# A long convolution and a linear attention on one core: transposes moved to DMA, paired 64-channel tails, and a new order of the work

## The chip, the core and the metric

The kernel runs on one core of a Trainium2 chip. The core has five engines with queues of their own: TensorE (PE in the profile, its weight loads PEld), VectorE (DVE), ScalarE (ACT), GpSimd (POOL) and SyncE (SP), which here only issues DMA. The metric is the device time of one execution in microseconds; less is better.

## The reference

Two independent blocks on 2048 positions and 576 channels, in bfloat16, whose outputs stand side by side in the last dimension.

```
# block A: a gated long convolution
k_shift = sum over t < 4 of k[s - t] * shift_k[:, t]
kv = k_shift * v
y = irfft(rfft(kv padded to 2S) * rfft(ssm_k padded to 2S))[:S] + kv * ssm_D
outA = q * y

# block B: linear attention with 32 heads of 18 channels
q, k, v = split(x @ wqkv)
phi(t) = where(t > 0, t + 1, exp(t)) + 1e-6
kv = einsum("bhsd,bhse->bhde", phi(k), v);  z = sum of phi(k) over s
o = einsum("bhqd,bhde->bhqe", phi(q), kv) / (phi(q) . z + 1e-6)
outB = o @ wo
```

## The kernel before

One string, `ORDER`, lists some 280 units of work, and the program issues them in that order. Each engine executes its own instructions in the order of issue, so the string fixes every engine's queue; semaphores hold an instruction back until its data and its buffers are there. A unit is a name with arguments and, last, the letters of the engines that take its elementwise steps (A for ACT, D for DVE, P for POOL): `cv.0.3.PDD` is convolution chunk 0, step 3, with its multiplication on POOL and the two other steps on DVE. All PSUM tiles share one pool of four buffers of two banks, taken in rotation.

Block A works in five chunks of channels (`ACH`: four of 128, one of 64).

- `hl` loads a chunk of the filter `ssm_k`; `hT` (L443) turns it with 16 TensorE transposes into PSUM, evicts it and adds `ssm_D` into row 0 (L448).
- `cv` (L427 to L433) is the four-tap shift convolution, elementwise in SBUF, and its product with v.
- A long DFT is split in two factors. `h1` and `u1` (L460) multiply by the tables G (filter and signal), evicted into Ch and Cu. `ht` and `ut` (L467) turn these by DMA into Cth and Ctu. `h2` and `u2` (L483) are the short factor, evicted into T and SU.
- `pX` and `pT` (L493, L495) are the complex product of the two spectra on DVE, whole tiles of 128 x 2048 with both inputs in SBUF.
- `i1` (L507) is the short inverse factor: two planes of T and two of X are multiplied by small tables W and added in PSUM, from two row halves. `i2` (L520, L521) is the long one with the tables F, and is multiplied by q on eviction (L522). F is G turned: `FT` (L529) is 16 TensorE transposes and an eviction for each of the two. `st` stores the result.

Block B works in four groups of 512 positions and 16 rows of 128 positions.

- `xd` loads x turned, by DMA transposes; `xl` loads it straight, for G below.
- `k` and `q` (L397, L406) are the projections followed by phi (L389 on ACT, L390 on DVE). q is kept turned, in five channel chunks `HCH` of whole heads: four of 126 channels, one of 72.
- `G` (L570) is x^T phi(k), 32 matmuls for each of five units; `kv` (L583) multiplies it by the weights of v and masks it to blocks of heads; `M` (L601) multiplies that by wo.
- `den` (L610) gives the denominators for all positions, and 1/den is taken on DVE. `bc` (L635) spreads 1/den over the channels by a matmul with a selection matrix (`es` makes it, masked for each group), and DVE multiplies q by it.
- `o` (L644) multiplies q by M: per row, five chunks, each a matmul of 512 and one of 64 columns; ACT evicts, and one DMA per row stores.

At the start `io`, `iw`, `wk`, `ix`, `sin`, `sw` compute index tables and sines; `wu.40` is 40 matmuls on zeros; `hc` makes masks on POOL.

Of the kernel before, what the change touches and what calls it, by code (L numbers as in the profile page):

```python
# [25 lines left out]

ACH = [(0, 128), (128, 128), (256, 128), (384, 128), (512, 64)]
# [3 lines left out]
wm io wu.0 ix.0 sin.1 id ix.1 hl.0 iw wk wu.40 sin.0 hT.0.D FT.1.D h1.0.0.0.A h1.0.1.0.A FT.0.D h1.0.1.1.A  # L31
h1.0.0.1.A iv sw W lw.0 xd.2 q.2.0 hc lw.1 k.8 q.2.2 q.2.1 ls Wj hl.1 hT.1.D k.9 k.11 k.10 h1.1.1.0.D xd.0 k.3
kl.0 cv.0.0.D one h1.1.0.0.A k.1 ht.0.0 h2.0.0.0.A h2.0.0.1.A eps cv.0.1.DD cv.0.2.DD q.0.1 h1.1.1.1.A q.0.0
h1.1.0.1.A xd.3 q.3.0 q.0.2 vl.0 cv.0.3.PDD k.2 cv.1.0.P k.0 ht.0.1 h2.0.1.1.A q.3.1 k.12 u1.0.1.1.A k.15
h2.0.1.0.D ht.1.1 h2.1.1.0.A k.13 u1.0.0.1.A hl.2 hT.2.D u1.0.0.0.A cv.1.1.PD k.14 xd.1 u1.0.1.0.A xl.2
cv.1.2.DD cv.1.3.DPP ht.1.0 xl.1 h2.1.1.1.A q.1.1 h2.1.0.1.A h2.1.0.0.A q.1.0 q.1.2 h1.2.1.0.A ut.0.1 k.7
u2.0.1.0.D u2.0.1.1.A k.6 h1.2.0.1.A k.4 ut.0.0 u2.0.0.1.D u2.0.0.0.A k.5 pX.0.0 pT.0.0 u1.1.1.0.A u1.1.1.1.A
q.3.2 u1.1.0.1.A xl.0 xl.3 kl.1 pX.0.1 pT.0.1 u1.1.0.0.A es G.0 vl.1 h1.2.0.0.A h1.2.1.1.A cv.2.0.D cv.2.1.DD
cv.2.2.DD G.2 ut.1.0 G.4 u2.1.0.1.D u2.1.0.0.A ut.1.1 i1.0.0.1.A hl.3 i1.0.0.0.A i1.0.1.1.A i1.0.1.0.A
cv.2.3.DDD ql.0 cv.3.0.D cv.3.1.DD u2.1.1.1.A ht.2.0 u2.1.1.0.A pX.1.1 pT.1.1 hT.3.A G.1 lwv pX.1.0 pT.1.0  # L40
h2.2.0.1.A ht.2.1 G.3 cv.3.2.DD u1.2.0.0.A i2.0.0 kl.2 u1.2.1.1.A u1.2.1.0.A kv u1.2.0.1.A i2.0.1 h2.2.0.0.A
h2.2.1.0.A den h2.2.1.1.A i1.1.1.0.A lwo M.0 i1.1.0.1.A i1.1.0.0.A i1.1.1.1.D ut.2.0 u2.2.0.0.A M.2 ut.2.1
# [23 lines left out]
def _warm(tc, psum, K, n):  # L66

    nc = tc.nc
    zero = K.sm[:, 1984:2048].bitcast(BF)
    if n:  # L70
        ps = psum.tile([128, 128], FP32, name="warm_ps", tag="big")
        for _ in range(n):
            nc.tensor.matmul(ps[:], lhsT=zero, rhs=zero, start=True, stop=True)
    else:
        nc.vector.memset(zero, 0.0)


def _head_consts(tc, cpool, K):
# [8 lines left out]
    K.hmask = cpool.tile([128, 7], FP32, name="hmask")  # L87
    nc.gpsimd.memset(K.hmask[:], 1.0)
    nc.gpsimd.affine_select(out=K.hmask[:], in_=K.hmask[:], compare_op=ALU.is_ge, fill=0.0, base=0,
                            pattern=[[-18, 7]], channel_multiplier=1)  # L90
    nc.gpsimd.affine_select(out=K.hmask[:], in_=K.hmask[:], compare_op=ALU.is_ge, fill=0.0, base=17,
                            pattern=[[18, 7]], channel_multiplier=-1)

    K.esel = cpool.tile([128, 5, 126], BF, name="esel")
    nc.gpsimd.memset(K.esel[:], 1.0)
    for j in range(4):
        e = K.esel[32 * j:32 * (j + 1)]
        nc.gpsimd.affine_select(out=e, in_=e, compare_op=ALU.is_ge, fill=0.0, base=0,
                                pattern=[[126, 5], [1, 126]], channel_multiplier=-18)
        nc.gpsimd.affine_select(out=e, in_=e, compare_op=ALU.is_ge, fill=0.0, base=17,  # L100
                                pattern=[[-126, 5], [-1, 126]], channel_multiplier=18)
    K.jmask = cpool.tile([128, 4], FP32, name="jmask")
    nc.gpsimd.memset(K.jmask[:], 0.0)
    for j in range(4):
        nc.gpsimd.memset(K.jmask[32 * j:32 * (j + 1), j:j + 1], 1.0)
# [126 lines left out]
def kernel(  # L232
# [24 lines left out]
    psum = ctx.enter_context(tc.tile_pool(name="psum", bufs=4, space=PSUM))  # L257
# [4 lines left out]

    def slot8(shape, dt, name):

        return c8.tile(shape, dt, name=name, tag="c8", bufs=2)

    def slotv(shape, dt, name):

        return c8.tile(shape, dt, name=name, tag="vq", bufs=2)
# [62 lines left out]
    Wall = slotv([128, D, 4], BF, "Wall")  # L332
    Wj = lpool.tile([128, 4, D], BF, name="Wj")
    pqT = lpool.tile([128, 5, S], BF, name="pqT")
    pk = big.tile([128, 16, D + 1], BF, name="pk", tag="pk")

    def load_shift():
        nc.sync.dma_start(out=Wall[:].rearrange("p d j -> p (d j)"),
                            in_=A_shift_k.rearrange("d j -> (d j)").partition_broadcast(128))

    def shift_w():
        nc.scalar.activation(out=Wj[:], in_=Wall[:].rearrange("p d j -> p j d"), func=ACT.Copy)
# [8 lines left out]
    def load_g(key, src, gi):  # L351
        d0, dn = GRP[gi]
        n = 19 if key == 'k' else 16
        if gi == 2:
            t = lpool.tile([128, n, dn], BF, name=key, tag="tail", bufs=2)
# [22 lines left out]
    def h_load(ci):  # L378
        d0, dc = ACH[ci]
        s = st.setdefault(ci, {})  # L380
        s['h'] = slot4([128, S], BF, "h_sb", "h", 2)
# [10 lines left out]
    def b_k(r):  # L392
        ps = psum.tile([128, 1024], FP32, name="k_ps", tag="big")
# [7 lines left out]
    def b_q(g, pair):  # L401
        ps = psum.tile([128, 2, 512], FP32, name="q_ps", tag="big")
        for j, c in enumerate(pair):
            h0, hn = HCH[c]
            for t in range(5):
                nc.tensor.matmul(ps[0:hn, j, :], lhsT=wqk[:, t, h0:h0 + hn], rhs=xT[g][:, t, :],  # L406
                                 start=(t == 0), stop=(t == 4))
        n = len(pair)
        hn = HCH[pair[0]][1]
        phi(ps[0:hn, 0:n, :], pqT[0:hn, pair[0]:pair[0] + n, g * 512:(g + 1) * 512], hn)  # L410
# [25 lines left out]
    def h_T(ci, eng='D'):  # L436
        d0, dc = ACH[ci]
        s = st[ci]
        h = s['h']
        ps = psum.tile([128, 16, 128], BF, name="hT_ps", tag="big")  # L440
        hv = h[0:dc, :].rearrange("d (a b) -> d b a", b=16)
        for b in range(16):
# [282 lines left out]
```

## Time and profile before

| | |
|---|---|
| median of three runs | 172.44 us (171.57 to 173.75) |
| the profiled execution, first to last instruction | 170.0 us |
| what lies around the span (median less span; the page gives the profiled execution no other time) | 2.4 us |
| PE busy | 159.0 us, 2176 matmuls |
| DVE busy | 139.7 us |
| ACT busy | 122.8 us |
| POOL busy | 70.9 us |
| DMA | 32.58 MB, mean 192 GB/s |

Busy time is the share of the span in which an engine works on something; a busy PE need not be at its peak, since matmuls overlap. An engine's idle time matters only where the end of the program waits for it.

### The profile page before, as it was taken

To read this page: it belongs to the slowest core of one execution; us is meant where nothing else is said; L and a number is where in the kernel's file an instruction comes from. 1 tells how busy PE (TensorE), PEld (TensorE's weight loads), DVE (VectorE), ACT (ScalarE), POOL (GpSimd) and SP (SyncE) were. 2 spreads that over 40 slices of the span, in tenths; PEclk is the share of its full clock that TensorE was granted. 3 is DMA by queue.
4 is the path that set the end of the run, shared out by engine and by line. 5 is a ranking of instruction groups with operands and counts; after the bars stand their busy time and mean duration, and the time that the engine had idled before them with its cause. 6 is when DMAs were issued, how large, how long until landed. Compare 5 with 4: busy or idle time off the path is not lost.

```text
span 170.0 us, 4984 instructions
## 1 busy us (share of the span) xinstructions
PE 159.0 (94%) x2176; PEld 106.9 (63%) x2176; DVE 139.7 (82%) x159; ACT 122.8 (72%) x142; POOL 70.9 (42%) x76
## 2 busy tenths in 40 slices
PE   4779999999999799999999999999999999999990
PEld 4768566665575456565685586857856765677750
DVE  7995589998989867999599887997999777999530
ACT  3458987977788899923597477989897778784431
POOL 7998982027693397000000049999900400000000
PEclk9999999999999999999999999999999999999997
DMA  5999699799989999999998655980959957988685
GB/s 147 273 268 250 119 267 136 137 272 225 145 183 217 263 178 318 290 213 219 306 214 196 106 150 40 182 159 18 146 126 276 202 128 69 237 180 258 191 244 117
DMA packets 81704, 32.58 MB, mean 192 GB/s; under 512 B 57432, under 2 KB 80978, under 8 KB 81682
## 3 DMA queue, kind: packets, MB, share of 16 engines
q1 hardware_dynamic: 81682, 32.26, 91.0%
q8 instruction: 17, 0.28, 0.7%
q14 instruction: 5, 0.04, 0.1%
HBM read 15.48 MB, written 4.72 MB: 119 GB/s over the span
## 4 chain that ended last, share of the span: by engine, by line
PE 77%; DMA 11%; DVE 6%; ACT 3%; issue 0%; ACTq 0%
PE q_ps L406 12%; PE g_ps L570 12%; PE k_ps L397 11%; PE o_ps L644 10%; PE s_ps L460 8%; PE i_ps L507 8%; DMA Ctu<-Cu 7%; PE s_ps L483 5%; DMA Cth<-Ch 4%; PE hT_ps L443 2%; PE i_ps L520 2%; PE i_ps L521 2%; PE bc_ps L635 1%; PE kv_ps L583 1%; DVE mp L138 1%; DVE mp L139 1%
## 5 line engine op out<-in xcount | busy, mean ns | idle before, releaser
L429 POOL TENSOR_TENSOR at<-k,Wj 128x2048 bf16<-128x2048 bf16 (+1 forms) x5 | 16.4, 3289 | 36.3 <-DVE at L430 36.2
L406 PE MATMUL q_ps<-xT,wqk 128*126 128x512 bf16 (+1 forms) x100 | 23.3, 381 | 0.0
L644 PE MATMUL o_ps<-wo_M,pqT 126*128 126x512 bf16 (+3 forms) x160 | 21.9, 286 | 0.0
L397 PE MATMUL k_ps<-wqk,xT 128*128 128x512 bf16 (+1 forms) x160 | 21.8, 286 | 0.0
L460 PEld LDWEIGHTS <-G 128*128 128x128 bf16 x320 | 17.6, 98 | 5.2 <-issue 2.1
L570 PE MATMUL g_ps<-pk,x_sb 128*128 128x512 bf16 (+3 forms) x160 | 20.4, 286 | 0.0
L277 ACT ACTIVATE Cu<-s_ps 128x1024 bf16<-128x1024 f32 (+1 forms) x18 | 16.6, 951 | 2.8 <-PE s_ps L460 2.4
L397 PEld LDWEIGHTS <-xT 128*128 128x128 bf16 x160 | 11.4, 98 | 11.1 <-issue 1.1
L644 PEld LDWEIGHTS <-pqT 126*128 126x128 bf16 (+1 forms) x160 | 11.2, 97 | 10.7 <-issue 0.8
L406 PEld LDWEIGHTS <-wqk 128*126 128x126 bf16 (+1 forms) x100 | 12.5, 131 | 8.2 <-issue 1.2
L277 ACT ACTIVATE Ch<-s_ps 128x1024 bf16<-128x1024 f32 (+1 forms) x18 | 16.3, 952 | 1.4 <-PE s_ps L460 0.8
L507 PE MATMUL i_ps<-W,T 64*128 64x128 bf16 x288 | 16.6, 216 | 0.4 <-DVE pqT L638 0.4
L649 ACT ACTIVATE ob<-o_ps 128x576 bf16<-128x576 f32 x16 | 10.4, 653 | 8.9 <-PE o_ps L644 8.7
L570 PEld LDWEIGHTS <-x_sb 128*128 128x128 bf16 (+1 forms) x160 | 10.8, 101 | 9.5 <-issue 0.2
L507 PE MATMUL i_ps<-W,X 64*128 64x128 bf16 x288 | 16.5, 216 | 0.0
L277 ACT ACTIVATE T<-s_ps 128x1024 bf16<-128x1024 f32 x16 | 15.8, 1021 | 0.6 <-PE s_ps L483 0.6
L277 ACT ACTIVATE V<-i_ps 128x1024 bf16<-128x1024 f32 x14 | 13.6, 1027 | 2.8 <-PE i_ps L507 2.1
L390 DVE SCALAR_TENSOR_TENSOR pqT<-pqT,q_ps 126x1024 bf16<-126x1024 bf16 (+1 forms) x12 | 12.2, 1037 | 3.8 <-ACT pqT L389 3.8
L522 DVE TENSOR_TENSOR q<-i_ps,q 128x1024 bf16<-128x1024 f32 (+1 forms) x10 | 11.2, 1116 | 4.6 <-PE i_ps L521 4.6
L389 ACT ACTIVATE pqT<-q_ps,neg 126x1024 bf16<-126x1024 f32 (+1 forms) x12 | 11.6, 968 | 4.3 <-PE q_ps L406 4.3
L430 POOL TENSOR_TENSOR at<-at 128x2048 bf16<-128x2048 bf16 (+1 forms) x4 | 12.4, 3094 | 5.4 <-DVE at L429 5.2
L433 POOL TENSOR_TENSOR v<-at,v 128x2048 bf16<-128x2048 bf16 (+1 forms) x3 | 10.3, 3419 | 9.8 <-DVE at L430 9.6
(120 smaller groups left out, 335.4 us busy)
## 6 DMA issues: line engine op xcount, KB each, us to landing
x_sb<-in_B_x_dram SPq DMA_DIRECT2D x4, 576.0 KB
out_dram<-ob SPq DMA_DIRECT2D x16, 144.0 KB, 4.0
h_sb<-in_A_ssm_k_dram SPq DMA_DIRECT2D x4, 512.0 KB
k<-in_A_k_dram SPq DMA_DIRECT2D x2, 1024.0 KB, 9.1
v<-in_A_v_dram SPq DMA_DIRECT2D x2, 1024.0 KB, 6.6
q<-in_A_q_dram SPq DMA_DIRECT2D x2, 1024.0 KB
out_dram<-q SPq DMA_DIRECT2D x2, 1024.0 KB
wqk<-in_B_wqkv_dram SPq DMA_DIRECT2D x2, 576.0 KB
```

The lines of the kernel that those rows point to most:

```text
L277: nc.scalar.activation(out=out, in_=in_, func=ACT.Copy)
L389: nc.scalar.activation(out=out_ap, in_=ps_ap, func=ACT.Exp, bias=K.neg1[0:n, :])
L390: nc.vector.scalar_tensor_tensor(out=out_ap, in0=out_ap, scalar=1.0, in1=ps_ap, op0=ALU.min, op1=ALU.max)
L397: nc.tensor.matmul(ps[:, n0:n1], lhsT=xT[r // 4][:, t, rr * 128:(rr + 1) * 128], rhs=wqk[:, t, D + n0:D + n1], start=(t == 0), stop=(t == 4))
L406: nc.tensor.matmul(ps[0:hn, j, :], lhsT=wqk[:, t, h0:h0 + hn], rhs=xT[g][:, t, :], start=(t == 0), stop=(t == 4))
L429: on[0].tensor_tensor(out=t_, in0=kk[:, 3 - stage:19 - stage], in1=wb(stage), op=ALU.mult)
L430: on[1].tensor_tensor(out=a_, in0=a_, in1=t_, op=ALU.add)
L460: nc.tensor.matmul(ps[:, bi, 0:dc], lhsT=K.G[ri][:, b, :], rhs=xf(b), start=True, stop=True)
L507: nc.tensor.matmul(ps[:, r, g, :], lhsT=s[key, hf][64 * r:64 * r + 64, z, x, 128 * g:128 * g + 128], rhs=K.W[64 * r:64 * r + 64, m, :], st ...
L522: nc.vector.tensor_tensor(out=qs, in0=ps[:, :, 0:dc], in1=qs, op=ALU.mult)
L570: nc.tensor.matmul(ps[0:fn, n0:n1], lhsT=x_sb[:, r, f0:f0 + fn], rhs=pk[:, r, n0:n1], start=(r == 0), stop=(r == 15))
L644: nc.tensor.matmul(ps[:, n0:n1], lhsT=pqT[0:hn, c, r * 128:(r + 1) * 128], rhs=B['M'][0:hn, c, n0:n1], start=(c == 0), stop=(c == 4))
```

## The change

It has seven parts.

1. **Transposes by DMA.** The two tables F are G turned by a DMA transpose. Filter chunks 1 to 4 are first copied with their axes swapped (new unit `hp`, on POOL for chunks 1, 3 and 4 and on ACT for chunk 2) and then turned by a DMA transpose; chunk 0 keeps the TensorE transposes.
2. **128-channel chunks of q.** q lies in four chunks of 128 channels and a tail of 64. The tails of two groups of positions share one tile of 128 partitions (`pq4`, unit `qt`): groups 2 and 0, and 3 and 1.
3. **Paired output.** `o` computes two rows at once; the tails of the two rows use the two halves of the partitions. One DMA stores both rows, and each row's eviction has an engine letter.
4. **32-row 1/den tiles.** `bc` reads only the 32 rows of 1/den that belong to a group of positions, and two groups sit on different row groups of TensorE; one unit `bt` serves the tails. The masked selection matrices (`es`) are gone.
5. **M with 128-channel chunks.** Heads cross chunk borders, so each of four chunks of M gets a second small product (`kvx`).
6. **Pre-subtracted products.** `pS` subtracts the second plane of T from the first, so that `i1` reads three planes and not four. It is used for chunks 2 and 3 (POOL three times, DVE once). `pX` and `pT` may run on POOL: seven of the 18 products do.
7. **Order and buffers.** `ORDER` is new throughout, and the digits behind a slash now name the PSUM buffer and the slots of SBUF rings that a unit takes, in place of a rotation. x for group 0 is the first load, then the weights; masks (`hc`) are made in the middle.

```diff
-    def b_q(g, pair):
-        for j, c in enumerate(pair):
-            h0, hn = HCH[c]
+    def b_q(g, half):
+        for j in range(2):
+            c = 2 * half + j
             for t in range(5):
-                nc.tensor.matmul(ps[0:hn, j, :], lhsT=wqk[:, t, h0:h0 + hn], rhs=xT[g][:, t, :],
+                nc.tensor.matmul(ps[:, j, :], lhsT=wqk[:, t, 128 * c:128 * c + 128], rhs=xT[g][:, t, :],
                                  start=(t == 0), stop=(t == 4))
...
+    def b_qt(p):
+        ps = psum.tile([128, 512], FP32, name="qt_ps")
+        for t in range(5):
+            for i, g in enumerate(PAIR[p]):
+                nc.tensor.matmul(ps[64 * i:64 * i + 64, :], lhsT=wqk[:, t, 512:576], rhs=xT[g][:, t, :],
+                                 start=(t == 0), stop=(t == 4))
+        phi(ps[:], pq4[:, p, :], 128)
...
+    def h_perm(ci, eng='P'):
+        s['hp'] = slot4([128, 16, 128], BF, "hp", "h", 3)
+        hv = s['h'][0:dc, :].rearrange("d (a b) -> d b a", b=16)
+        if eng == 'A':
+            nc.scalar.activation(out=s['hp'][0:dc], in_=hv, func=ACT.Copy)
+        else:
+            (nc.gpsimd if eng == 'P' else nc.vector).tensor_copy(out=s['hp'][0:dc], in_=hv)
+
+    def h_T(ci, eng='T'):
+        if eng == 'T':
+            s['hT'] = slot4([128, 16, 128], BF, "hT", "h", 3)
+            nc.sync.dma_start_transpose(out=s['hT'][:, :, 0:dc], in_=s['hp'][0:dc].rearrange("d b a -> d (b a)"))
+        else:
...
-    def prod(ci, hf, key):
+    def prod(ci, hf, key, eng='D'):
+        e = nc.gpsimd if eng == 'P' else nc.vector
...
+            a = t if key == 'S' else s['X', hf]
+            e.tensor_tensor(out=a[:, :, 0, :], in0=a[:, :, 0, :], in1=a[:, :, 1, :],
+                            op=ALU.subtract if key == 'S' else ALU.add)
...
+        planes = [('T', 0, 0)] + [('T', 1, 1)] * ('S' not in done) + [('X', 0, 2)] + [('X', 1, 2)] * ('A' not in done)
...
-        for b in range(16):
-            nc.tensor.transpose(out=ps[:, b, :], in_=K.G[ri][:, b, :], identity=K.ident[:])
-        evict(K.F[ri][:], ps[:], eng)
+        nc.sync.dma_start_transpose(out=K.F[ri][:], in_=K.G[ri][:].rearrange("p b k -> p (b k)"))
...
+        for i in range(2):
+            j = 2 * gg + i
+            q = slice(32 * j, 32 * j + 32)
+            nc.tensor.matmul(ps[:, i, :], lhsT=K.esel[q, 128 * c:128 * c + 128], rhs=B['rden'][q], start=True, stop=True)
...
+    def b_out(p, rr, eng='AA'):
+        rs = [4 * g + rr for g in PAIR[p]]
...
+        for n0, n1 in ((0, 512), (512, 576)):
+            for i in range(2):
+                h = slice(64 * i, 64 * i + 64)
+                nc.tensor.matmul(pss[i][:, n0:n1], lhsT=pq4[h, p, rr * 128:(rr + 1) * 128], rhs=B['M'][h, 4, n0:n1],
+                                 start=False, stop=True)
+        for i, r in enumerate(rs):
+            evict(B['ob'][:, r, 0:D], pss[i][:, 0:D], eng[i])
```

The new order, from the masks to the end of block A's third chunk, reads (each unit's buffers behind the slash):

```diff
+h2.1.0.1.D/31 h2.1.0.0.D/0 lwv hT.2.T/2 ut.1.1/0 G.4/20 pT.0.1.P h1.2.1.0.A/13 ut.1.0/1 h1.2.1.1.A/1 h1.2.0.0.A/0
+cv.3.0.D FT.1 pT.0.0.D pS.1.1.N cv.3.1.PD wom kv/23 h1.2.0.1.A/1 ql.0/1 u2.1.1.0.A/10 u2.1.0.1.D/02 u2.1.0.0.A/3 den/1
+u2.1.1.1.A/0 i1.0.1.0.A/02 i1.0.0.0.A/3 i1.0.0.1.A/0 ht.2.1/1 i1.0.1.1.A/2 h2.2.1.0.A/13 pX.1.1.D/0 cv.3.2.PP ht.2.0/0
...
+hT.3.T/0 h2.2.0.1.A/01 h2.2.0.0.A/2 i2.0.0/3 h1.3.1.1.A/01 lwo bc.3.1/0 M.0.A/2 ut.2.0/1 h1.3.1.0.A/3 h1.3.0.1.D/1
+pT.1.1.P h1.3.0.0.A/2 M.3.D/0 u2.2.0.0.A/13 hl.4/21 ut.2.1/0 bc.1.1/1 pT.1.0.P u2.2.0.1.A/2 bt/0 M.4.A/3 M.1.A/1
+cv.3.3.DDD M.2.A/2 u2.2.1.1.A/03 u2.2.1.0.A/0 ht.3.1/1 ht.3.0/0 i1.1.1.1.D/11 i1.1.0.0.A/2 i1.1.1.0.A/3 hp.4.P/1
...
```

293 lines of the change are left out of this document (158 added, 135 removed).

## The prediction

> **What bounds the kernel now.** I read the page from the top: busy time by engine, the 40 slices, the DMA queues, the chain that ended last.
>
> ```profile
> span 170.0 us, 4984 instructions
> PE 159.0 (94%) x2176; PEld 106.9 (63%) x2176; DVE 139.7 (82%) x159; ACT 122.8 (72%) x142; POOL 70.9 (42%) x76
> PEclk9999999999999999999999999999999999999997
> GB/s 147 273 268 250 119 267 136 137 272 225 145 183 217 263 178 318 290 213 219 306 214 196 106 150 40 182 159 18 146 126 276 202 128 69 237 180 258 191 244 117
> DMA packets 81704, 32.58 MB, mean 192 GB/s; under 512 B 57432, under 2 KB 80978, under 8 KB 81682
> PE 77%; DMA 11%; DVE 6%; ACT 3%; issue 0%; ACTq 0%
> ```
>
> PE is busy 94% and holds 77% of the chain, so TensorE sets the end. The stretches of 10 us (columns: stretch, length, then busy time of PE, PEld, DVE, ACT, POOL) say where it waits: 0.87, 0.82 and 0.48 us here, 2.2 in all between 20 and 160.
>
> ```profile
> 50.00:60.00 10.00, 9.13 (x84) 5.39 (x83) 8.81 (x9) 8.28 (x9) 4.80 (x3) 1.00 1.22 231
> 110.00:120.00 10.00, 9.18 (x116) 6.11 (x114) 8.61 (x9) 8.82 (x12) 9.77 (x5) 1.00 0.55 107
> 130.00:140.00 10.00, 9.52 (x196) 7.13 (x190) 7.83 (x9) 7.16 (x9) 2.12 (x1) 1.00 1.12 190
> ```
>
> A matmul's own duration overlaps its neighbours, so I take prices from the chain (start, length, what), where groups stand end to end:
>
> ```profile
> 12.56 1.07 PE s_ps L460 x16
> 13.63 0.89 PE ft_ps L529 x16
> 15.41 2.18 PE q_ps L406 x10
> 17.59 1.23 PE k_ps L397 x10
> 22.06 0.99 PE hT_ps L443 x16
> 62.43 1.33 PE k_ps L397 x10
> 104.19 1.19 PE den_ps L610 x19
> 119.58 0.25 PE m_ps L601 x2
> 121.19 1.11 PE hT_ps L443 x16
> 123.75 1.23 PE o_ps L644 x10
> 133.33 0.50 PE bc_ps L635 x2
> 148.01 3.72 PE i_ps L507 x128
> 165.78 0.65 ACT ob L649
> ```
>
> TensorE's unbroken stream runs from 12.56 to 165.8; 4.2 us of eviction and output follow. The page gives this execution no time but its span; the median of the runs is 172.44, so 2.4 us lie around the span, and I add them.
>
> **The change, TensorE first.** Two things are read off the chain before any price. Matmuls on different column groups run side by side: the 32-wide 512-column ones of `den` cost 1.19/19 = 0.063 us, against 0.216 for a full one (2.18/10). Row halves do too: `i1` costs 3.72/128 = 0.029, against 0.056 for a 128-column one (0.89/16).
> - q: 100 full matmuls become 80, and 20 of 64 columns in pairs, worth 10: 10 x 0.216 = 2.2 saved.
> - Output: two rows cost 2 x 1.23; four chunks of five stay (1.97) and the tails pair (0.25). 8 x (2.46 - 2.21) = 2.0 saved.
> - 1/den broadcast: ten units of about 0.5 become nine whose two matmuls sit on different row groups, about 0.27: 2.6 saved.
> - Transposes: four filter chunks (0.99 to 1.11, 4.3 together) and one table (0.89) leave the stream; the other table was turned before 12.56. The first chunk's transposes, done before 12.56 now, come into it: +1.0. Net 4.2 saved.
> - `i1` of chunks 2 and 3, eight units of 0.93: a quarter of the matmuls goes, 1.9 saved.
> - M: four chunks get a second pair of matmuls of 0.25: 1.0 lost.
>
> Net 11.9. After `s2`, which uses small tiles, k takes 1.33 and not 1.23: 0.1 for a change of tiling. Some 19 new small-tile groups bring such changes; bounds 0 and 2, I take 1.0. Stream: 10.9 shorter.
>
> **The start.** x for the first group goes first now, then the weights:
>
> ```profile
> 2.72 3.57 SPq L312 DMA_TRANSPOSE xT<-in_B_x_dram  x1
> 6.34 1.25 SPq L313 DMA_TRANSPOSE xT<-in_B_x_dram  x1
> 10.27 5.96 SPq L312 DMA_TRANSPOSE xT<-in_B_x_dram  x1
> wqk<-in_B_wqkv_dram SPq DMA_DIRECT2D x2, 72.0 KB, 4.7
> k<-in_A_k_dram SPq DMA_DIRECT2D x2, 1024.0 KB, 9.1
> Cth<-Ch SPq DMA_TRANSPOSE x9, 5.9
> 2.40 4.45 PE L73 MATMUL warm_ps<-sm 128*128 128x128 bf16 x40 [2.40 <-DVE sm L75]
> 7.84 1.86 PE L443 MATMUL hT_ps<-ident,h_sb 128*128 128x128 bf16 x16 [1.00 <-DVE ident L62]
> ```
>
> Issued at 0.8, x takes 4.9 us of queue; the weights' second part leaves near 6 and lands 4.7 later: k can begin near 10.4 (8.5 to 11.5), 2.2 before 12.56. But nothing stands between the 40 warming matmuls, which end near 5.6, and k. The 40 took 0.11 each and the 16 after them 0.116, twice the later 0.056, although the granted clock is printed at full: TensorE starts slow. Before, that slow stretch lay in waiting time; now k and q pay it. Doubled for about 4.4 us it costs 2.2 (0 to 4). Start: 0 in sum. The Trainium skill, "TensorE: Matmul & The Clock Gate", section "What's actually happening", has the array at half clock until a 3.4 us window was busy and again after an idle one; by it I would estimate 1.7 here in place of 2.2.
>
> Waits: the filter's path is now load, permuting copy (POOL or ACT), DMA transpose, a one-row add on DVE, and behind that add stand the phi operations of k. A transpose between SBUF tiles lands in 5.9 us (median of Cth). I put 1.0 for all new waits, between -2 (none of the present ones left) and 8. TensorE's line: 170.0 - 10.9 + 1.0 + 2.4 = 162.5.
>
> **The other engines.** On DVE sixteen operations of 1.22 go (tables, filters, products, two convolution steps) and nine come (evictions that ACT loses, two products with v); of the shorter ones, near 0.69, seven more come than go, and the four mask products go (1.5): 140 - 8.5 + 4.8 - 1.5 = 135. ACT has less to do. POOL gains seven products of 4.07 and three copies: 71 becomes about 106. The rows behind these prices, and why POOL's part matters:
>
> ```profile
> 25.63 0.21 DVE L448 TENSOR_TENSOR hT<-hT,Drow 1x128 bf16<-1x128 bf16 x1
> 48.13 4.08 POOL L429 TENSOR_TENSOR at<-k,Wj 128x2048 bf16<-128x2048 bf16 x1
> 51.86 0.43 DVE L448 TENSOR_TENSOR hT<-hT,Drow 1x128 bf16<-1x128 bf16 x1
> 121.21 2.13 POOL L430 TENSOR_TENSOR at<-at 128x1024 bf16<-128x1024 bf16 x1
> 123.06 0.33 DVE L448 TENSOR_TENSOR hT<-hT,Drow 1x64 bf16<-1x64 bf16 x1
> L493 DVE TENSOR_TENSOR X<-SU,T 128x2048 bf16<-128x2048 bf16 x9 | 10.9, 1217 | 0.5 <-ACT T L277 0.4
> L427 DVE TENSOR_TENSOR at<-k,Wj x3: 1215/1217/1225, 30.0 to 88.4; 128x2048 bf16<-128x2048 bf16 x3
> L495 DVE TENSOR_TENSOR T<-SU,T x9: 1214/1224/1226, 70.0 to 156.0; 128x2048 bf16<-128x2048 bf16 x9
> L98 POOL TENSOR_SCALAR_AFFINE_SELECT esel<-esel 32x630 bf16<-32x630 bf16 x4 | 2.9, 736 | 0.2
> L430 DVE TENSOR_TENSOR at<-at 128x1024 bf16<-128x1024 bf16 x1 | 0.7, 691 | 0.0
> ```
>
> The one-row add takes 0.21 alone. Started while POOL multiplies, it ends at 52.29, 0.08 behind POOL's 52.21, and the other at 123.39, 0.05 behind 123.34: a DVE operation with two SBUF inputs stood still until POOL's was done. So I count both engines' two-input work on one line, from the first convolution product to the last product of T. Before: POOL 8 x 4.07 + 6 x 2.13, DVE 42 x 1.22 + 2 x 0.69, 98 us in the 127 from 30.0 to 157.2: 77% full. After: POOL 15 x 4.07 + 6 x 2.13 = 73.83, DVE 35 x 1.22 + 6 x 0.69 = 46.84: 120.7. It cannot start before k lands: 19 us of issues ahead of it (x twice, 12 us; weights, filters, shift, 4; k's own parts, 2.6) and 9.1 to landing, near 28.5. Behind its end TensorE still owes 7.2 (two `i1` 1.9, two output units 4.4, the last `i2` 0.9), then 4.2. Quite full, 28.5 + 120.7 + 7.2 + 4.2 + 2.4 = 163.0.
>
> The two lines end together, 162.5 and 163.0; with two such lines each waits now and then for the other, and I add 1.5: **164.5**.
>
> **Rivals.**
> - The shared line is longer and decides. Place: the 20 us run of four POOL products and a convolution ahead of `cv.3.3`, and the last products. POOL's eight selects of 0.74, the other masks (2) and three permuting copies (2 each, unseen; 0.7 to 4.07) now lie inside the stretch, 14 us. If they hold DVE off as well: 177.0, slower. It decides from a fill of 92%: at 120.7/0.92 = 131 the end is where it is today. For it: 77% now. Against it: 135 - 47 = 88 us of DVE's work have at most one SBUF input, and can run while POOL works. Chance 0.20, half of it ending short of 175.9. The Trainium skill, "SBUF — State Buffer", section "SBUF: two separate sides", calls the DVE/GpSimd port pair an exclusive lock held for a whole instruction; the two adds agree.
> - The shared line hardly binds, as the two engines' turns are set by the data anyway: 162.5 or less. It lies in the forecast's range.
> - DVE becomes the bound with its idle (170.0 - 139.7) unchanged: 135 + 30.3 + 2.4 = 167.7. For it: 8.8 of 10 busy in the middle already. Against: part of that idle is the drained end, where nothing was left for it. 0.10, half of it above 169.
> - The pairs don't run side by side, so the change doesn't do what it says: 2.2 + 2.0 + 2.4 come back: 171.1. 0.04.
> - DMA: six more transposes, 2.9 MB. At the present mean of 192 GB/s, 35.5 MB take 185: 187.3. It decides under 222 GB/s, which 160 us need; the first 20 slices average 221. 0.04, because the later slices, as low as 18, show want of work and no limit.
>
> **How the numbers follow.** Forecast 0.62. Faster by over 2% (under 169.0; 2% is about what a measurement of this kernel tells from no change): 0.62 + half of DVE's 0.10 = 0.67. Within 2%: the other 0.05, half of the shared line 0.10, pairs 0.04: 0.19. Slower: 0.10 + 0.04 = 0.14. Range: low end, TensorE's line with an early start and no slow clock, 162.5 - 5 = 157.5; high end 175, which takes in DVE and half the shared line. The forecast's own range is 157.5 to 169.
>
> **What would show it.** q, output, broadcast and `i1` groups at the prices above; no `ft_ps`, 16 `hT_ps`. k starting near 10.4 at 0.43 a full matmul for some 4 us. POOL near 106 busy; DVE's two-input operations over 1.22, or idle before them released by POOL, between 85 and 150. TensorE's idle well above 2.2 there, beside a full POOL, would mean that the shared line decides; idle at `s2` released by DMA would mean the queue. Wrong altogether if `i1`'s waits for POOL's products push the end past 172.

## The result, and the profile after

The changed kernel takes 190.88 us (median, 190.24 to 192.09) where the kernel before took 172.63 beside it: a ratio of 1.107, with a 95% interval of 1.100 to 1.114. It is **18 us slower**; 164.5 was forecast. Where the executions of a kernel below fell into a faster and a slower group, its time here is the median of the faster group (a single execution for e1, e16 and e18), while the profiles of e1, e2, e9, e12, e16 and e18 are of slower executions.

The page of the changed kernel, the lines that answer to those of before:

```profile
span 190.4 us, 4683 instructions
PE 159.2 (84%) x2009; PEld 98.4 (52%) x2027; DVE 157.6 (83%) x157; ACT 114.4 (60%) x127; POOL 116.4 (61%) x85
PEclk9889969999999978999966995899999999589998
DMA packets 93031, 35.45 MB, mean 186 GB/s; under 512 B 68760, under 2 KB 92306, under 8 KB 93010
PE 18%; DVE 10%; POOL 3%; issue 2%; ACT 1%; DVEq 0%; ACTq 0%
```

The chain of waits breaks off here (its shares sum to 34%), so I read the span by stretches instead. TensorE is busy as long as before (159.0), although work was taken from it, and idles 31.2 us instead of 11.0 (18 of its 2027 matmuls have no record in this trace, so the idle time is somewhat overstated). VectorE, which was to fall to 135, is busy 157.6. The third line shows the second half of the riddle: the clock granted to TensorE drops again and again. Five of the 10 us stretches (busy time of PE, PEld, DVE, ACT, POOL, then granted clock, DMA share, GB/s):

```profile
20.00:30.00 10.00, 7.50 (x55) 3.99 (x53) 9.93 (x10) 4.85 (x6) 4.42 (x2) 0.83 0.91 211
90.00:100.00 10.00, 5.90 (x66) 4.07 (x65) 9.41 (x10) 4.21 (x5) 5.04 (x3) 0.84 0.63 162
100.00:110.00 10.00, 9.97 (x237) 6.52 (x237) 7.51 (x15) 7.52 (x9) 8.59 (x3) 0.82 0.66 109
110.00:120.00 10.00, 6.13 (x69) 4.42 (x69) 8.98 (x6) 5.19 (x7) 8.84 (x3) 0.69 0.48 119
160.00:170.00 10.00, 8.01 (x95) 5.82 (x96) 7.88 (x9) 3.62 (x5) 4.24 (x2) 0.66 0.31 82
```

Where TensorE idles, VectorE is busy for 7.9 to 9.9 of the 10 us and GpSimd for 4.2 to 8.8, and in the same stretch or the next one the clock is low. Multiplying TensorE's busy time by the granted clock, stretch by stretch, and summing gives its work at full speed. The span then splits into three terms:

| kernel | work at full speed | lost to a lower clock | idle | span |
|---|---|---|---|---|
| before | 158.5 | 0.5 | 11.0 | 170.0 |
| changed | 147.1 | 12.1 | 31.2 | 190.4 |

So by this trace 11.4 us of work were saved (the kernels e11 and e12 below have the same matmuls with every record, and give 10.2 and 9.7), and 20.2 of idle time and 11.6 of clock were added. What TensorE waited for (total, times, longest):

```profile
PE s_ps L495 <- DVE v L455: 5.6, 2, 3.4
PE s_ps L495 <- DVE hT L483: 4.8, 2, 2.5
PE s_ps L495 <- DVE pqT L682: 3.7, 1, 3.7
PE k_ps L413 <- DMA wqk<-in_B_wqkv_dram: 3.6, 1, 3.6
```

Past the start, the great waits are for VectorE. The groups of VectorE's operations say why it is late (busy, mean ns, idle before):

```profile
L452 DVE TENSOR_TENSOR at<-at 128x2048 bf16<-128x2048 bf16 x10 | 16.3, 1630 | 0.2
L530 DVE TENSOR_TENSOR X<-SU,T 128x2048 bf16<-128x2048 bf16 x5 | 9.7, 1945 | 0.3 <-ACT SU L292 0.2
L532 DVE TENSOR_TENSOR T<-SU,T 128x2048 bf16<-128x2048 bf16 x6 | 7.2, 1212 | 0.0
L483 DVE TENSOR_TENSOR hT<-hT,Drow 1x128 bf16<-1x128 bf16 x4 | 7.1, 1769 | 0.0
```

A product of this shape takes 1212 ns where it runs alone (T); of the five X, four took 1.22 to 1.25 us and one 4.81, which makes the mean of 1945. The one-row add, 0.21 us alone, takes 1.77 in the mean. The timelines of GpSimd, VectorE and TensorE (start, length) show single cases:

```profile
73.02 1.60 POOL L107 TENSOR_SCALAR_AFFINE_SELECT esel<-esel 32x576 bf16<-32x576 bf16 x1
75.39 0.66 POOL L107 TENSOR_SCALAR_AFFINE_SELECT esel<-esel 32x576 bf16<-32x576 bf16 x1
...
83.58 4.58 POOL L532 TENSOR_TENSOR T<-SU,T 128x2048 bf16<-128x2048 bf16 x1
85.38 3.88 DVE L451 TENSOR_TENSOR at<-k,Wj 128x2048 bf16<-128x2048 bf16 x1
...
109.07 4.05 POOL L530 TENSOR_TENSOR X<-SU,T 128x2048 bf16<-128x2048 bf16 x1 [1.33 <-PE i_ps L552]
109.40 4.81 DVE L530 TENSOR_TENSOR X<-SU,T 128x2048 bf16<-128x2048 bf16 x1
114.13 1.21 DVE L682 SCALAR_TENSOR_TENSOR pqT<-pqT,bc_ps 128x1024 bf16<-128x1024 bf16 x1
...
155.47 4.05 POOL L530 TENSOR_TENSOR X<-SU,T 128x2048 bf16<-128x2048 bf16 x1
155.55 4.53 DVE L452 TENSOR_TENSOR at<-at 128x1024 bf16<-128x1024 bf16 x1 [1.55 <-POOL at L451]
160.11 0.69 DVE L455 TENSOR_TENSOR v<-at,v 128x1024 bf16<-128x1024 bf16 x1
160.85 0.89 PE L495 MATMUL s_ps<-v,G 128*128 128x64 bf16 x24 [3.44 <-DVE v L455]
```

Read the last four together. GpSimd starts a product at 155.47; VectorE's addition of 0.69, started 0.08 later, lasts 4.53 and ends 0.56 behind it; the product that gives v follows, and TensorE, which needs v, has waited 3.44. At 109.40 the same happens to a product, and behind it in VectorE's queue stands the 1/den product (L682) whose PSUM buffer TensorE waits 3.70 for. It goes both ways: GpSimd's select takes 0.66 alone and 1.60 beside VectorE, its product 4.58 instead of 4.06.

### The profile page after: what moved, and what is told of

Same layout as the page of the kernel before. It is cut to its first block, busy times and chain, and to the rows that moved or that the text cites. A ratio compares the mean times of both kernels' runs of the same rounds, so it can differ in the third digit from the quotient of the medians.

```text
span 190.4 us, 4683 instructions
## 1 busy us (share of the span) xinstructions
PE 159.2 (84%) x2009; PEld 98.4 (52%) x2027; DVE 157.6 (83%) x157; ACT 114.4 (60%) x127; POOL 116.4 (61%) x85
## 2 busy tenths in 40 slices
DMA packets 93031, 35.45 MB, mean 186 GB/s; under 512 B 68760, under 2 KB 92306, under 8 KB 93010
## 5 line engine op out<-in xcount | busy, mean ns | idle before, releaser
L451 POOL TENSOR_TENSOR at<-k,Wj 128x2048 bf16<-128x2048 bf16 (+1 forms) x8 | 29.1, 3635 | 10.8 <-DVE at L452 6.5
L495 PEld LDWEIGHTS <-G 128*128 128x128 bf16 x320 | 19.4, 105 | 20.3 <-issue 11.2
L413 PE MATMUL k_ps<-wqk,xT 128*128 128x64 bf16 (+1 forms) x155 | 22.5, 292 | 4.6 <-DMA wqk<-in_B_wqkv_dram 3.6
L452 DVE TENSOR_TENSOR at<-at 128x2048 bf16<-128x2048 bf16 (+1 forms) x12 | 21.5, 1792 | 1.8 <-POOL at L451 1.6
L610 PE MATMUL g_ps<-pk,x_sb 128*128 128x65 bf16 (+3 forms) x156 | 21.5, 292 | 0.9 <-ACT Cu L292 0.5
L495 PE MATMUL s_ps<-v,G 128*128 128x128 bf16 (+1 forms) x160 | 11.9, 235 | 10.2 <-DVE v L455 5.6
L530 POOL TENSOR_TENSOR X<-SU,T 128x2048 bf16<-128x2048 bf16 x4 | 16.2, 4061 | 6.1 <-PE i_ps L552 6.1
L422 PE MATMUL q_ps<-xT,wqk 128*128 128x512 bf16 x78 | 19.3, 397 | 0.1
L703 PE MATMUL o_ps<-wo_M,pqT 128*128 128x64 bf16 (+1 forms) x121 | 17.1, 283 | 1.3 <-DVE q L567 0.8
L610 PEld LDWEIGHTS <-x_sb 128*128 128x128 bf16 (+1 forms) x160 | 11.3, 103 | 11.7 <-issue 3.1
L406 DVE SCALAR_TENSOR_TENSOR pk<-pk,k_ps 128x576 bf16<-128x576 bf16 x16 | 11.8, 749 | 4.8 <-ACT pk L405 4.7
L552 PE MATMUL i_ps<-W,T 64*128 64x128 bf16 x224 | 14.8, 217 | 0.2
L466 POOL COPY hp<-h_sb 128x2048 bf16<-128x2048 bf16 (+1 forms) x3 | 11.7, 3904 | 5.1 <-DMA h_sb<-in_A_ssm_k_dram 5.1
L452 POOL TENSOR_TENSOR at<-at 128x2048 bf16<-128x2048 bf16 (+1 forms) x3 | 10.3, 3420 | 6.6 <-DVE at L451 5.3
```

Of the source, the lines that this page charges most:

```text
L406: nc.vector.scalar_tensor_tensor(out=out_ap, in0=out_ap, scalar=1.0, in1=ps_ap, op0=ALU.min, op1=ALU.max)
L413: nc.tensor.matmul(ps[:, n0:n1], lhsT=xT[r // 4][:, t, rr * 128:(rr + 1) * 128], rhs=wqk[:, t, D + n0:D + n1], start=(t == 0), stop=(t == 4))
L422: nc.tensor.matmul(ps[:, j, :], lhsT=wqk[:, t, 128 * c:128 * c + 128], rhs=xT[g][:, t, :], start=(t == 0), stop=(t == 4))
L451: on[0].tensor_tensor(out=t_, in0=kk[:, 3 - stage:19 - stage], in1=wb(stage), op=ALU.mult)
L452: on[1].tensor_tensor(out=a_, in0=a_, in1=t_, op=ALU.add)
L466: (nc.gpsimd if eng == 'P' else nc.vector).tensor_copy(out=s['hp'][0:dc], in_=hv)
```

## The experiments

The runs are called by the number ahead of their label. **Theory**: a GpSimd operation that reads SBUF and a VectorE operation with two SBUF inputs exclude each other, VectorE's queue behind the held operation stands still with it, and TensorE then loses idle time and, after it, clock. **Rivals**: the new order leaves TensorE waiting whoever does the work; the new units or the filter's path by DMA cost; VectorE simply has too much to do. Units are named as in the order string: a last letter P, D or A is GpSimd, VectorE or ScalarE, T a transpose by DMA, N left undone.

**1. What GpSimd's work costs by itself, in the kernel before.** Five products more from 67 us, where GpSimd idled; against them ten fills.

```diff
 vl.1
+ds      # 5 x gpsimd.tensor_tensor(out=d, in0=Wj[0:2048], in1=Wj[256:2304])   (e3)
+ds      # 10 x gpsimd.memset(d, 0)                                            (e4)
```

> The kernel before with five products of two SBUF tiles of 2048 more on GpSimd (20.3 us; result unused), from about 67 us, where GpSimd is idle and VectorE 8 to 10 of 10 busy. Theory: VectorE operations of 1.22 there are stretched to 2 to 4 us, GpSimd's own to over 4.1, and the end comes 8 to 16 later: 180.5 to 188.5. Rival (GpSimd's work beside VectorE costs nothing by itself): 171.5 to 174.

> The same place and about the same GpSimd time (ten fills of 2048 at about 2 us, estimated from 0.73 for 768) but with nothing read from SBUF. Theory (it is the reading of operands that excludes): no VectorE operation stretched, 171.5 to 174. Rival (any GpSimd work that touches SBUF holds VectorE): as the run with five products, 180 or more.

Measured: 191.09 with the products (1.109, 1.101 to 1.117), 176.30 with the fills (1.023, 1.014 to 1.032). The timeline with products:

```profile
68.91 23.52 POOL L670 TENSOR_TENSOR dose<-Wj 128x2048 bf16<-128x2048 bf16 x5 [2.16 <-PE q_ps L405]
69.46 4.96 DVE L494 TENSOR_TENSOR T<-SU,T 128x2048 bf16<-128x2048 bf16 x1
74.94 4.48 DVE L492 TENSOR_TENSOR X<-SU,T 128x2048 bf16<-128x2048 bf16 x1
84.33 9.01 DVE L626 TENSOR_SCALAR esel<-esel,jmask 128x630 bf16<-128x630 bf16 x4
```

and with fills:

```profile
69.88 18.80 POOL L670 MEMSET dose<- 128x2048 bf16 x10 [1.79 <-PE q_ps L405]
73.44 1.23 DVE L494 TENSOR_TENSOR T<-SU,T 128x2048 bf16<-128x2048 bf16 x1
74.58 6.77 DVE L626 TENSOR_SCALAR esel<-esel,jmask 128x630 bf16<-128x630 bf16 x4
```

Five products, 20.3 us by their length alone and 23.5 here, cost 18.5 us of time, and the products of VectorE beside it take 4.5 to 5.0 instead of 1.22. Fills leave those at 1.23. With the products, TensorE's one great wait is for an eviction that needs a small VectorE copy queued behind the held operations:

```profile
PE g_ps L569 <- ACT wv_GT L573: 14.6, 1, 14.6
```

Both runs came out above what the theory gave them (191.1 for at most 188.5, 176.3 for 174). The fills cost 3.7 (2.4 to 5.5). The only VectorE operations that took longer beside them are the four mask products, which have one SBUF tile as input and take 1.26 together in the kernel before, and the same wait of TensorE is 2.7 there; that this is the whole of the 3.7 was not tried.

```profile
74.18 1.26 DVE L627 TENSOR_SCALAR esel<-esel,jmask 128x630 bf16<-128x630 bf16 x4
```

**2. The parts of the change undone or moved, in its own order.**

```diff
-pT.0.1.P pX.1.0.P pT.1.1.P pT.1.0.P pX.2.0.P pX.2.1.P pX.3.1.P
+pT.0.1.D pX.1.0.D pT.1.1.D pT.1.0.D pX.2.0.D pX.2.1.D pX.3.1.D     (e1, e2, e5)
-hp.1.P hp.3.P hp.4.P      -hc (at 67 us)         -pS.*.P pS.*.D
+hp.1.A hp.3.A hp.4.A      +hc (behind W)         +pS.*.N            (e2)
-hp.* hT.1.T hT.2.T hT.3.T hT.4.T
+hT.1.D hT.2.D hT.3.A hT.4.D                                         (e5, e6)
```

> The changed kernel with its seven GpSimd products (4.07 us each there) on VectorE (1.22 each). Theory (a GpSimd operation that reads SBUF and a VectorE operation with two SBUF inputs hold each other up): 28.5 us of such GpSimd time go, VectorE gets 8.5 of work and yet its busy time falls from 157.6 to under 155, TensorE waits less and its busy time falls below 156; 178 to 185 us. Rival 1 (the order and the filter's path by DMA are to blame, the products are harmless): 189 to 192, VectorE busy about 166. Rival 2 (VectorE simply has too much to do): slower than 190.9, 193 to 198.

> As the run before, and also the three permuting copies on ScalarE, the masks built near the start (ahead of the first convolution) and no product subtracted ahead (two more planes in i1, TensorE gets 1.9 back). GpSimd then reads SBUF for the convolutions alone, as in the kernel before. Theory: held operations nearly vanish (first products of a convolution, 128x2048, back to a mean under 1.4), VectorE busy under 146, 171 to 178 us. Rival 1 (order and the DMA path of the filter): 187 to 192. Rival 2 (VectorE overloaded): 190 or more.

> The changed kernel with its filters of chunks 1 to 4 turned by TensorE again (no permuting copies, no transposes of them by DMA), the seven products on VectorE, the masks near the start and nothing pre-subtracted: GpSimd reads SBUF for the convolutions alone and neither it nor ScalarE copies. TensorE has 4.3 + 1.9 more than in the changed kernel. Theory (GpSimd's exclusions, and the copies of 3.9 us in two in-order queues): TensorE is the bound again, 169 to 177, its busy time 153 to 157 and its mean clock over 0.97. Rival (the order itself leaves TensorE waiting whoever does the work): 183 to 192 with TensorE's idle over 25.

 (masks and subtractions as in e2)

> The changed kernel with the filters of chunks 1 to 4 turned by TensorE again and nothing else undone: the seven products, the masks and the subtractions stay on GpSimd. Theory (exclusions first): 184 to 190, a gain of what the three copies on GpSimd and the one on ScalarE held up, less 4.3 on TensorE. Rival (the filter's path by DMA is the cause): 172 to 180.

Measured: e1 183.87, e2 188.29, e5 189.09, e6 193.80. e1 lies in the range of the theory, but by a single execution, so it decides nothing. The other three are slower than the theory gave them, and e2 and e5 lie in the ranges of their rivals. In e2 VectorE is hardly held (busy 143.8), but ScalarE has 12 us of copies more, two of them back to back, and TensorE idles 26.5 and loses 12.6 to the clock. In e5 and e6 TensorE waits for PSUM buffers ahead of the transposes put back (2.7 and 2.2 us at two of them in e5). So far the rival "the order" stood as well as the theory. These runs move work from one full engine to another and can't tell them apart.

**3. The changed code in the old order.**

```diff
-q.2.2 q.0.2 q.1.2 q.3.2   bc.4.0 bc.4.1   o.0 to o.15
+qt.0 qt.1                  bt              o.0.0 to o.1.3
-FT.1.D FT.0.D (by TensorE, at the start)
+FT.0 FT.1 (by DMA, behind vl.1)                                                            (e7, e9)
+qt.0 ahead of xd.3; bc.2.1 bc.1.1 bc.3.1 between o.3's place and o.0.0                     (e7)
+qt.0 behind k.3; bc.2.1 bc.1.1 bc.3.1 ahead of o.0.0, spread                               (e9)
-pT.0.1 pX.1.0 pT.1.1 pT.1.0 pX.2.0 pX.2.1 pX.3.1
+pT.0.1.P pX.1.0.P pT.1.1.P pT.1.0.P pX.2.0.P pX.2.1.P pX.3.1.P                             (e8, on e7)
```

> The changed code (128-channel chunks, paired tails, 32-row 1/den tiles, tables turned by DMA) in the order and on the engines of the kernel before: filters turned by TensorE, all products on VectorE, nothing pre-subtracted, tiles placed in turn; the two halves of the 1/den products come before the first output, which needs both now. By the prediction's prices TensorE saves 2.2 + 2.0 + 2.6 + 0.9 and loses 2.0. Theory (the code is sound, engines and order cost the time): 165 to 172, TensorE busy 152 to 155. Rival (something in the new units themselves, pairs or 32-row tiles, costs): 175 or more.

> As the run before, with the same seven products on GpSimd as in the changed kernel and nothing else moved. Theory (each 4.07 us product on GpSimd keeps VectorE's operations on SBUF tiles waiting; five of them cost the kernel before 18.5 us at a place where VectorE was full): 10 to 25 over the run before. Rival (harmless, GpSimd has idle time): within 3 of it, or faster, as VectorE is rid of 8.5.

> The changed code in the old order a second time, without the three places that the last such run left TensorE waiting at: the first tail pair of q right after the k unit of its second x group (its x is free again for the fourth group), the 1/den products of the second half spread over the places ahead of the first output, the two output pairs where three outputs were. Engines as in the kernel before. Theory (the TensorE savings are real, and idle time above that of the kernel before is what the new order and the GpSimd work cost): TensorE busy 152 to 156, idle 11 to 16, 164 to 172. Rival (the new units need so much more waiting that no order near the old one holds them): 176 or more.

Measured: e7 191.29, e8 210.41, e9 181.39; e7 and e9 are as slow as their rivals had them. e7 waits 4.8 us for x of the fourth group, whose load now stands behind the tail pair, and 4.5 ahead of an output; with these mended, e9 saves 4.7 us of TensorE's work (153.8 at full speed) and idles 23.7: 3.6 us of it for the table G at the start (1.2 in the kernel before), 3.4 for transposes by DMA, the rest in smaller places. So the changed units did not fit the old order in these two tries. What can be used is the difference of e8 and e7, in which nothing but the engine of seven products differs: 19.1 us, where the theory had 10 to 25.

**4. The clock: work put into waits.**

```diff
+wz.40  h1.0.0.0.A      # 40 identity matmuls ahead of the unit, into its own PSUM tile
+wz.36  u1.1.0.1.A
+wz.36  h1.2.0.0.A
+wz.50  u1.4.0.1.A
```

> The changed kernel with matmuls on the identity (128x128, about 0.056 us each; their result is overwritten) ahead of four s1 units that wait for data: 40 where it waits 2.5 us at 25, 36 at 69 (2.1), 36 at 96 (2.3), 50 at 160 (3.4). They fill waits and add 9 us to TensorE's work if they ran at full speed. Theory (an idle TensorE is granted a lower clock for the next microseconds, so idle time costs twice): the granted clock in the stretches 20 to 30, 70 to 80 and 160 to 170 rises from 0.83, 0.86 and 0.66 to over 0.95, and the kernel comes out 2 to 5 faster than the changed one, 186 to 189, although it does more. Rival (the lower clock costs nothing, or is not set by idleness): 190.5 to 194.

Measured: 187.78 (1.096, 1.091 to 1.102), 3.1 faster than the changed kernel with 9 us more to do. Set against the kernel before, which was run beside each, the gain is 1.8 us, and the two intervals touch (1.100 to 1.114 for the changed kernel). Three stretches where matmuls were put in, and a fourth without any:

```profile
20.00:30.00 10.00, 9.93 (x106) 6.54 (x106) 9.90 (x11) 6.51 (x8) 4.45 (x2) 1.00 0.96 227
70.00:80.00 10.00, 9.29 (x101) 5.40 (x100) 9.59 (x9) 6.41 (x4) 9.45 (x10) 1.00 1.17 260
160.00:170.00 10.00, 8.74 (x188) 6.31 (x189) 8.99 (x10) 6.71 (x10) 4.25 (x2) 1.00 0.49 134
120.00:130.00 10.00, 10.00 (x118) 5.05 (x112) 7.85 (x7) 5.93 (x7) 3.24 (x2) 0.50 0.50 111
```

The clock is 1.00 where it was 0.83, 0.86 and 0.66, and the loss over the span falls from 12.1 to 7.9. So the low clock follows from the waits; that it costs time of its own is likely from this run, but the gain is small beside the intervals. Of the 7.9, 5.0 lie in the fourth stretch: behind a wait of 1.87 us at 114.6 the clock stays at 0.50 although TensorE is busy throughout. How long a low clock lasts can't be read from the length of the wait.

**5. GpSimd's added work without its reading.** These were the runs that decided. The work keeps its place in the order and, in e12, nearly its length, but reads one column in place of all, so these kernels leave out the products, copies and masks that they fill.

```diff
-e.tensor_tensor(out=X, in0=SU, in1=T, op=mult)            # 4.07
+e.tensor_tensor(out=X[..., 0:1], in0=SU[..., 0:1], ...)    # one column
+e.memset(X, 0.25)   # once in e11, for X and the copies only; twice in e12
```

> The changed kernel in its own order with what the change gave GpSimd left out: its seven products, its four subtractions and the four permuting copies (one of them on ScalarE) touch one column in sixteen or fewer, with the X products and the copies replaced by one fill of 1.9 us, and the masks' selects are dropped. No other engine does that work instead. GpSimd falls from 116 to about 75 busy. Theory (GpSimd's added work, by exclusion and by its own length, is what costs): 168 to 176, TensorE idle under 18. Rival (the order leaves TensorE waiting anyway): 181 or more.

> The changed kernel in its own order with GpSimd's added work at its old length but as fills that read nothing: each product of 4.07 us is one column of it and two fills of 1.9, each copy on GpSimd likewise, each select a fill; the copy on ScalarE stays. Theory (VectorE is held up by the exclusion): VectorE's operations of two SBUF inputs are back near 1.22 outside the convolutions' time, 172 to 180. Rival 1 (it is the length of GpSimd's queue that makes i1 and the filters late): 186 to 192. Rival 2 (the order alone): 181 to 186, within 3 of the run before.

> The changed kernel with its seven GpSimd products alone as fills of the same length (one column is still multiplied); the copies, the masks' selects and the subtractions read SBUF as in the changed kernel. All of it as fills gave 167.3. Theory A (each operation that reads costs by its length; products 28.5 of some 45 us): 174 to 180. Theory B (the products alone decide, the others lie where VectorE has other work): 166 to 170.

> The counterpart: the three copies, the selects and the subtractions on GpSimd as fills of the same length, the seven products real. Theory A (by length): 178 to 185. Theory B (products alone decide): 188 to 192.

Measured: e11 166.52 (0.965, 0.954 to 0.976), e12 166.31 (0.962, 0.953 to 0.971), both faster than the theory had them; e13 176.25, e14 184.16, both within what a price by length gave. The page of e12, and three of its groups on VectorE (L446, L545 and L482 are the changed kernel's L452, L530 and L483):

```profile
span 167.5 us, 4728 instructions
PE 153.3 (92%) x2027; PEld 94.2 (56%) x2027; DVE 138.5 (83%) x157; ACT 114.5 (68%) x127; POOL 106.9 (64%) x111
DMA packets 93031, 35.45 MB, mean 212 GB/s; under 512 B 68760, under 2 KB 92306, under 8 KB 93010
...
L446 DVE TENSOR_TENSOR at<-at 128x2048 bf16<-128x2048 bf16 x10 | 12.2, 1221 | 0.2
L545 DVE TENSOR_TENSOR X<-SU,T 128x2048 bf16<-128x2048 bf16 x5 | 6.4, 1278 | 0.3 <-ACT SU L286 0.2
L482 DVE TENSOR_TENSOR hT<-hT,Drow 1x128 bf16<-1x128 bf16 x4 | 4.4, 1094 | 0.0
```

GpSimd is busy 106.9 and TensorE idles 14.2. With the same order, the same transposes and the same megabytes the kernel is 24.6 us faster once GpSimd's added work stops reading. The fills also change the numbers that TensorE multiplies; in e3 and e4 nothing uses the result of the added work, and there the reading makes 14.8 us. So the exclusion is shown to be the cause, and the order by itself, the new units, the DMA and the length of GpSimd's queue (e12 is no slower than e11) are not. Of the 24.6, the products alone account for 14.6 (190.9 to 176.3), the copies, selects and subtractions alone for 6.7 (to 184.2); 3.2 come only with both.

**6. Is there a better place for the work?** Whole kernels (e15, e16), and two in which some of GpSimd's work is a fill (e17, e18).

```diff
-pX/pT.*.P  pS.*.P  hp.*.P hp.2.A   hc (at 67 us)
+pX/pT.*.D  pS.*.D  hp.*.D          hc (behind W)                 (e15)
+pX/pT.*.D  pS.*.D  (hp as it was)  hc (behind W)                 (e16)
+pX/pT.*.D  pS.*.D  hp.*.D          masks by fills, at 67 us       (e17)
+pX/pT.*.D  pS, hp, masks by fills, in their places                (e18)
```

> A whole kernel: products, copies and subtractions on VectorE, the masks near the start; GpSimd reads SBUF for the convolutions alone. VectorE then has the 138 of the run with fills, and 8.5 for products, about 9 for copies (estimated from 2048 elements at one a cycle, some 2.1 to 3 us each, the one from ScalarE too) and 1.4 for subtractions: 157 to 158, more than 90% of any span below 174. Theory (VectorE is then the bound with the idle of some 20 us that it had in the changed kernel and in the one before): 176 to 184. Rival (only exclusion matters, the order hides the rest): 167 to 172, faster than both kernels.

> As the run before with the copies where the changed kernel has them (three on GpSimd, one on ScalarE). VectorE about 148 and what three copies of 3.9 us hold up. Theory: 174 to 182, since 20 us of idle remain on VectorE and the copies cost up to 8. Rival (copies hurt as much as their length and more, through the filter they deliver late): 183 or more.

> As the run with products, copies and subtractions on VectorE (191.6), with the masks left at their place in the changed order and built by fills. Theory (VectorE is the bound once it has 16 us more: each microsecond given to it costs one or more, as TensorE's waits cost clock as well): 183 to 190. Rival (the masks moved to the start were what made that run slow, VectorE has room): 168 to 178.

> The changed kernel with the copies, selects and subtractions on GpSimd as fills and the seven products real on VectorE, 8.5 us of work there, where the same kernel with the products on GpSimd took 184.2 and with the products as fills 167.3. Theory (VectorE is full: 8.5 to 17 us for 8.5 of work): 176 to 184, hardly better than on GpSimd. Rival (without exclusion VectorE has room for them): 167 to 173.

Measured: e15 189.42, e16 188.79, e17 191.00, e18 173.26. e15 and e16 were forecast too fast (e16 as its rival has it), e17 came out just above its theory, and e18 between its rival (up to 173) and its theory (from 176), again by a single execution. Moving the masks was not what made e15 slow. The page of e17:

```profile
PE 161.5 (85%) x2009; PEld 98.5 (52%) x2027; DVE 156.6 (83%) x171; ACT 111.1 (59%) x126; POOL 61.4 (32%) x72
```

VectorE is as busy as in the changed kernel, now with work of its own in place of holds: 18.1 us more than in e12 cost 24.7. The seven products alone are 8.5 us on VectorE and cost 7.0 (e18 against e12, by the one execution); on GpSimd they cost 17.9 (e14 against e12). So VectorE has little room in this order. None of the whole kernels is faster than the one before.

## Why the prediction was wrong, step by step

**TensorE's stream: right in the sum, partly by luck.** 10.9 us were to go, about 10 went at full speed (11.4 by the changed kernel's trace, 9.7 and 10.2 by e12 and e11). The chain of waits shows the prices (start, length):

```profile
128.87 0.32 PE m_ps L643
129.19 0.32 PE m_ps L645
129.51 0.14 PE m_ps L643
129.65 0.13 PE m_ps L645
...
134.01 0.34 PE bc_ps L680 x2
...
174.02 0.32 PE o_ps L703
174.39 1.69 PE o_ps L703 x14
176.08 0.35 PE o_ps L708 x4
```

The two broadcast matmuls do run side by side (0.34, forecast 0.27). The output pair takes 2.41 (174.02 to 176.43) and not 2.21, so that it saves 0.4 in eight and not 2.0. A chunk of M takes 0.91 (the first four lines) and not 0.50, so that M costs 2.6 and not 1.0. That the sum still came out comes from other parts, among them the 1.0 set aside for tilings; which ones was not traced. The rival that the pairs don't work falls.

**The start: better than forecast.** TensorE's timeline there:

```profile
8.74 2.56 PE L413 MATMUL k_ps<-wqk,xT 128*128 128x512 bf16 x10 [3.57 <-DMA wqk<-in_B_wqkv_dram]
11.46 1.17 PE L413 MATMUL k_ps<-wqk,xT 128*128 128x512 bf16 x9 [0.17 <-issue]
```

k begins at 8.74, not 10.4, and the slow clock holds for one unit (1.4 lost), not for 4.4 us of them. The second is luck: with the same start, e12 has a clock of 0.78 from 10 to 20 us and TensorE busy throughout, 2.2 lost.

**The shared line: this step failed.** The mechanism was named, with the two adds as evidence; its length was wrong. "Quite full" put 120.7 us of two-input work end to end from 28.5, with 1.5 us for mutual waiting. The first of these operations starts at 27.8 and the last product ends at 176.4: that is 148.6 us, 27.9 more. Laid over each other, the timelines of GpSimd and VectorE show where these went. An operation of the line (one of GpSimd's that reads SBUF, or one of VectorE's with two SBUF inputs) runs in 132.0 of the 148.6 us. The 11.3 us above 120.7 are mostly copies, selects and one-row adds, which the sum had left to a rival. In the other 16.6 us the line stands empty, its next operation waiting for data or behind other work in its queue; the sum had 1.5 for that, although the kernel before has 29.6 empty us in its 127.2. So the line did fill up, from 77% to 89%, and to 96% between 43.4 and 107.7 us, but never to 100%. With 148.6 in place of 120.7 the same sum gives 28.5 + 148.6 + 7.2 + 4.2 + 2.4 = 190.9. That this is the median to the digit is luck: behind the last product come 14.0 us and not 11.4, and around the span lie 1.7 (192.09 less 190.4) and not 2.4.

Against the rival I had argued that 88 us of VectorE's work have at most one SBUF input and can run meanwhile. Much of it does: of the 96.5 us in which GpSimd reads, VectorE spends 51.5 on such work. But in 33.0 of them it has a two-input operation open, mostly a held one, where the kernel before has 0.6 of 45.2: its order kept the two apart, and the new one does not. VectorE takes its queue in order, and what stands behind a held operation stands still with it, as at 109.40. That is also why the holds appear as busy time: VectorE is busy 157.6, and 138.5 when GpSimd's added work doesn't read (e12); the forecast of 135 was near the latter.

**The rival was the case, and too cheap.** I gave 0.20 to the shared line deciding, with the masks and copies in it, and 177.0 for it. The 14 us for masks and copies were about right (11.3 came onto the line, though a copy takes 3.9 on GpSimd and not 2), but again they were laid end to end, without the 16.6 empty us. e14 and e13 show both parts: products 14.6, the rest 6.7.

The Trainium skill, "SBUF — State Buffer", section "SBUF: two separate sides", says that a VectorE operation with two SBUF inputs is locked out only against a GpSimd operation that reads SBUF; the products at 1.23 beside fills and at 4.96 beside products agree.

**The clock: priced at the start alone.** "New waits +1.0" was a price for TensorE's idle time, and idle time has a second price: here 20.2 us of it came with 11.6 of clock. It is no fixed rate: in e3, where 15.5 us were added, nearly all in the one wait of 14.6, the clock cost 2.5 more. The Trainium skill, "TensorE: Matmul & The Clock Gate", section "What's actually happening", has the array fall back to half clock after an idle window of about 3.4 us; the 0.66 behind the wait of 3.44 agrees, while the 0.83 behind one of 2.50 shows that shorter waits can cost too. No run here measures the length of that window.

**The other rivals.** DMA at 192 GB/s as the limit falls: e12 moved the same 35.45 MB at 212. VectorE as the bound was right in that it has little room (e17), but its idle time was not what decided. What was to show the shared line as the bound is there in part: between 85 and 150 TensorE idles 10.2 us (1.3 before). GpSimd is not full there, at 43.5 of the 65 us; the line of both engines nearly is, at 58.9.

**What is left open.** TensorE's line alone was to give 162.5; e12 gives 166.3, with 14.2 of idle and 4.4 of clock in its profile, and convolutions that still exclude. How much of these 4 us is due to the convolutions on GpSimd was not tried. In e5 GpSimd reads for the convolutions alone and nobody copies, and yet it takes 189.1; which of the moved work costs these 23 us more than e12 is not shown. Nor is it shown whether another order of the changed code, with the products on VectorE, beats the kernel before.

## What to carry to other kernels

An offload from VectorE to GpSimd is not priced by what VectorE is rid of: while GpSimd reads SBUF, VectorE's two-input operations and everything queued behind them stand still, so 8.5 us of VectorE's products became 28.5 of exclusion and 15 to 18 us of time (e13 and e14). Where two engines share something, put everything on the line that excludes, add the empty time that the line has today, and ask of every held instruction what is queued behind it. And count TensorE's idle time with the clock that can follow it: here 20.2 us of waiting came with 11.6 of clock, in e3 15.5 with 2.5.

## What the runs showed of the hardware that was not expected

- Fills on GpSimd, which read nothing, leave VectorE's two-input products alone (1.23) and yet hold a one-input product on an SBUF tile: four of them took 6.77 instead of 1.26.
- A held operation counts as busy on its engine. VectorE's 157.6 held about 19 us of standing still (138.5 in e12); the comparison of one form's mean with its length alone shows it.
- GpSimd is held as well: selects of 0.66 took 1.5 to 1.6, a product of 4.06 took 4.58.
- After a wait of 1.87 us the granted clock stayed at 0.50 from 118 to 130 us in e10, with TensorE busy throughout.
- A permuting copy of 128x2048 takes 3.90 us on GpSimd, 3.95 on ScalarE and 2.05 on VectorE; a fill of that size 1.81 to 1.88 on GpSimd.
